# GpSimd is asked first for three steps of the first eight weight pieces, with 40 unread transpositions and new planner constants

## The chip, the cores and the metric

One core of one Trainium2 chip runs the kernel. The metric is the device time of one execution in microseconds (us), the median of three runs.

## What is computed

An attention with a decay bias, a network with a squared relu, and a network that takes the maximum of three products. All of it is done at float32 accuracy.

```python
def _attn_ref(q, k, v, s):                       # q, k, v: 4 x 8 x 576 x 64
    scores = scale * np.matmul(q, k.transpose(0, 1, 3, 2))
    cum = np.cumsum(np.maximum(s, 0.0), axis=-1)
    bias = -(cum[:, :, :, None] - cum[:, :, None, :])
    scores = np.where(causal, -1000000000.0, scores + np.minimum(bias, 0.0))
    attn = np.exp(scores - np.max(scores, axis=-1, keepdims=True))
    attn = attn / (np.sum(attn, axis=-1, keepdims=True) + 1e-09)
    return np.matmul(attn, v)

def _moe_ref(x, w_in, w_out, s, b):              # 2304 x 512, 512 x 2048, 2048 x 512
    r = np.maximum(x @ w_in, 0.0)
    return (s * (r * r) + b) @ w_out

def _moe2_ref(x, w1, w2, w3, w_out):             # three 512 x 768, then 768 x 512
    return np.maximum(np.maximum(x @ w1, x @ w2), x @ w3) @ w_out
...
x = attn_out.transpose(0, 2, 1, 3).reshape(B * S, H * D)
return _moe2_ref(_moe_ref(x))                    # 2304 x 512
```

## The kernel before

**Arithmetic.** TensorE multiplies float32 in a fast form (fp32r) that keeps only part of the digits. A number x is therefore held as a high part and a low part, and a product is three matmuls (L286 to L288: high x high, high x low, low x high). Attention scores of the first two kinds of jobs are made in plain float32 (L581, L583).

**Weights.** They come as 64-bit floats. `weight_steps` (L300) turns a piece of 128 rows into a high and a low float32 tile in nine steps: 0 the load (L311, SP's queue), 1 a scaling of the upper 32-bit words (L316, on ScalarE), 2 and 3 bit operations (L319, L321, VectorE), 4 the rounding to the high part (L275 or L277, ScalarE or VectorE), 5 and 6 bits and product of the lower words (L325, L327, VectorE), 7 a difference (L282) and 8 a sum that gives the low part (L331). Steps 7 and 8 are done on VectorE or GpSimd. The first network's weights in 14 pieces (name "a") are staged in tiles `wg`, `stage` and `wst`; the first eight, 384 columns wide, make `wa_in`, the other six, 512 wide, make `wa_out`.

**Attention.** Jobs of two heads: four jobs A (first 320 rows), four jobs B (the other 256), then whole pairs (W). For each block of rows: scores into PSUM (`ps`, L581/L583, later L591), a minimum on VectorE that also copies the scores to `pp` (L602), the exponential on ScalarE (L608), transpositions of `pp` on TensorE (`pt`, L680), copies of `pt` out of PSUM (L275 on ScalarE, L279 on VectorE), the product with v (`px`, L699), and a product with reciprocal sums (L707). The result `x` is split in high and low (L275, L282) for the first network, whose matmuls (L286 to L288) run in the same time as the attention. Each job needs its q and k (`raw`, L513), a one-hot row (`oh`, L571, on GpSimd), and the decay table (`dd`, L562; `dm`, L482, L484, L277, L275, saved by L493 and L494).

**Order.** Every engine runs its own list of instructions in a fixed order. A planner in the kernel (`Plan`) makes these lists at build time: it walks through the steps in an assumed time, gives each engine the ready step of the lowest priority, and takes a step's costs, its due time and the landing of loads from the constants at the top of the file. A step whose costs are a table of engines goes to the first engine named, unless another would end it earlier by `LATE_0` (`LATE` later in the plan, `LATE_F` for urgent steps). `convert` (L918) lists the steps of a weight piece; its due times are `W_1`, `W_S1`, `W_2` and `W_S2` with `W_AT`.

**Unread transpositions.** `warm` (L547) issues 30 transpositions of the identity before the first data come. `keep` (L553) is a step of the lowest priority, one transposition into a bank of PSUM that nobody reads; the planner puts it where TensorE has no other step. `KEEPS` of them exist, 56.

Of the kernel before, what the change touches and what calls it, by code (L numbers as in the profile page):

```python
# [8 lines left out]
F32 = mybir.dt.float32  # L9
# [4 lines left out]
AF = mybir.ActivationFunctionType  # L14
# [18 lines left out]
KEEP = 1  # L33
KEEPS = 56
VIA = 4
# [12 lines left out]
TURN = -6.0  # L48
LEAST = -0.257
EXP = 0.52  # L50
D_T = 1.77
P_HI = 0.517
R_AT = 0.543
D_AV = 5.833
# [3 lines left out]
AV = {"A": ((0, 1, 2),), "B": ((0, 1, 2), (3, 4)), "W": ((0, 1, 2), (3, 4))}  # L58
W_1 = -2.561
W_S1 = 4.286  # L60
W_2 = 29.555
W_S2 = 1.679
WG = (0, 1, 2, 5, 6)
WX = (7, 10, 13)
WB_1 = 116.522
WB_S = 8.739
WO_AT = 0.055
W_AT = (0, 2.0, 2.3, 2.8, 2.9, 3.3)
SLACK = 0.039
LATE = 0.898  # L70
LATE_F = 1.001
LATE_0 = 0.158
BUSY = 150
# [3 lines left out]
FAR_R = 0.846  # L77
FAR_Q = 0.818
LOADED = (60, 260)
# [4 lines left out]
TURN_C = 0.08  # L84
AV_C = 0.002
TURNS = ("turn_p", "turn_r")
# [140 lines left out]
def fused_kernel(ctx, tc, q, k, v, s, w_in, w_out, ms, mb, w1, w2, w3, w_fin, out,  # L227
                 f_split=6):
    nc = tc.nc
# [23 lines left out]
    scale = 1.0 / float(D) ** 0.5  # L253
# [46 lines left out]
    def weight_steps(piece, stage_tile):  # L300
# [10 lines left out]
        nc.sync.dma_start(st.bitcast(I64), src)  # L311
        yield
        word = lambda dt, i: st.bitcast(dt).rearrange("p (n t) -> p n t", t=2)[:, :, i]
        a = stage_tile(step, "wsa")
        lo = a.bitcast(F32R) if lo is None else lo
        nc.scalar.activation(a, word(F32, 1), AF.Copy, scale=2.0 ** -112)  # L316
        yield
# [600 lines left out]
    def convert(name, z, piece, stage_tile, prios, needs, ring_st, ring_a, **k):  # L918

        state = []  # L920

        def step(on=None):
            if not state:
                state.append(side_steps(piece) if name == "s" else weight_steps(piece(), stage_tile))
                next(state[0])
            else:
                state[0].send(on)

        n = piece.n
        either2 = {"DVE": dve(n), "Pool": pool_(n)}  # L930
        shift, either = dve_fast(n) - 0.06, {"Pool": pool_(n), "DVE": dve(n)}
        back = [("save", z)] if name == "s" else [("savef", z, 0), ("savef", z, 1)] if name == "f" else [("w", name, z, 8)]
        parts = (("SP", (1, 2 * n), (), [(ring_st, back)]), ("ACT", act(n), (0,), [(ring_a, back)] if ring_a else []),
                 ("DVE", shift, (1,), []), ("DVE", dve(n), (2,), []), ({"ACT": act(n), "DVE": dve_fast(n) - 0.06}, 0, (3,), []),
                 ("DVE", shift, (4,), []), ("DVE", dve(n), (5,), []), (either2, 0, (6,), []), (either2, 0, (7,), []))
        for i, (engine, cost, after, take) in enumerate(parts):
            if name in ("a", "s") and i == 1:
                cost += 0.05
            if name == "s":
                if engine == "DVE":  # L940
                    cost += 0.05
                elif isinstance(engine, dict) and "DVE" in engine:
                    engine = engine | {"DVE": engine["DVE"] + 0.05}
            add(("w", name, z, i), engine, cost, prios[min(i, len(prios) - 1)], [("w", name, z, j) for j in after] + (needs if not i else []), step, take=take,
                **(k | {"delay": 1.0} if name == "f" and not i else k))
# [14 lines left out]
    for z, piece in enumerate(all_a):  # L960
# [12 lines left out]
        t = W_1 + z * W_S1 if z < 4 else W_2 + (z - 4) * W_S2  # L973
        convert("a", z, piece, stage_a, [t + d for d in W_AT], [], "wg" if z in WG else "wx" if z in WX else "ws", None, att=True)

# [326 lines left out]
    def word(q, x, dt, i):  # L1302
        return wsts[q, x].bitcast(dt).rearrange("p (n t) -> p n t", t=2)[:, :, i]
# [393 lines left out]
```

## Time and profile before

| | us |
|---|---|
| median of 3 runs | 864.92 |
| lowest and highest | 864.79, 864.97 |
| the profiled execution | 864.14 |
| its span | 862.4 |
| busy TensorE (PE) | 853.8 |
| busy VectorE (DVE) | 633.7 |
| busy ScalarE (ACT) | 473.4 |
| busy GpSimd (POOL) | 333.4 |

The profile shows one execution. Its times are in us from the start of the span unless ns is written. A line number is that of the kernel; helpers such as `copy` (L275 to L279) and `minus` (L282) have one line for many uses, so the tiles' names tell the uses apart. An instruction's length overlaps with the next one's start by some 0.1 us, so what an instruction takes from its engine is better read from one start to the next. The granted clock of TensorE is at its full level, 2.4 GHz, in every stretch shown.

### The profile page before, as it was taken

To read this page: it belongs to the slowest core of one execution; us is meant where nothing else is said; L and a number is where in the kernel's file an instruction comes from. 1 tells how busy PE (TensorE), PEld (TensorE's weight loads), DVE (VectorE), ACT (ScalarE), POOL (GpSimd) and SP (SyncE) were. 2 spreads that over 40 slices of the span, in tenths; PEclk is the share of its full clock that TensorE was granted. 3 is DMA by queue.
4 is the path that set the end of the run, shared out by engine and by line. 5 is a ranking of instruction groups with operands and counts; after the bars stand their busy time and mean duration, and the time that the engine had idled before them with its cause. 6 is when DMAs were issued, how large, how long until landed. Compare 5 with 4: busy or idle time off the path is not lost.

```text
span 862.4 us, 15613 instructions
## 1 busy us (share of the span) xinstructions
PE 853.8 (99%) x5064; PEld 769.4 (89%) x5064; DVE 633.7 (73%) x1554; ACT 473.4 (55%) x1175; POOL 333.4 (39%) x353
## 2 busy tenths in 40 slices
PE   8999999999999999999999999999999999999998
PEld 7678989888888999999988888889998999989996
DVE  7999799878787789859599896454668366836650
ACT  7988998999885444726264462551236223532221
POOL 3536676687635222705041241410228122702220
PEclk9999999999999999999999999999999999999999
DMA  7664756656753576665759686428885255615502
GB/s 215 196 195 129 236 179 193 216 163 199 241 162 126 166 235 213 199 217 169 231 158 298 204 290 216 138 94 307 315 295 202 89 169 180 221 74 171 171 25 74
DMA packets 111336, 163.25 MB, mean 189 GB/s; under 512 B 11048, under 2 KB 62616, under 8 KB 111256
## 3 DMA queue, kind: packets, MB, share of 16 engines
q1 hardware_dynamic: 111016, 161.98, 58.1%
q8 instruction: 41, 0.67, 0.3%
q14 instruction: 39, 0.32, 0.1%
q10 hardware_dynamic: 240, 0.28, 0.1%
HBM read 117.79 MB, written 44.43 MB: 188 GB/s over the span
## 4 chain that ended last, share of the span: by engine, by line
PE 94%; DVE 3%; DMA 1%; ACT 1%; issue 0%; SPq 0%; ACTq 0%; DVEq 0%
PE mm L286 26%; PE mm L288 26%; PE mm L287 26%; PE pt L680 6%; PE px L699 5%; PE ps L591 5%; PE ps L581 1%; DMA wst<-in_moe_w_in_dram 1%; DVE pp L602 1%; PE pr L628 0%; DMA s<-in_s_dram 0%; SPq L513 0%; DVE stage L282 0%; DMA raw<-in_q_dram 0%; ACT pp L608 0%
## 5 line engine op out<-in xcount | busy, mean ns | idle before, releaser
L282 POOL TENSOR_TENSOR gbl<-g,gbh 128x512 fp32r<-128x512 f32 (+1 forms) x50 | 64.1, 1282 | 146.5 <-ACT gbh L275 143.5
L1141 ACT ACTIVATE g<-g 128x512 f32<-128x512 f32 (+4 forms) x86 | 48.3, 561 | 77.5 <-DVE g L1137 77.2
L608 ACT ACTIVATE pp<-pp,mn 64x64 f32<-64x64 f32 (+4 forms) x160 | 88.3, 553 | 4.4 <-DVE mn L602 4.1
L282 POOL TENSOR_TENSOR set<-raw,set 64x384 fp32r<-64x384 f32 x72 | 76.3, 1085 | 23.7 <-PE ps L591 6.3
L286 PE MATMUL mm<-ty,sdp 128*128 128x384 f32 x252 | 84.3, 335 | 0.0
L288 PE MATMUL mm<-ty,sdp 128*128 128x384 f32 x252 | 84.3, 335 | 0.0
L287 PE MATMUL mm<-ty,sdp 128*128 128x384 f32 x252 | 84.3, 334 | 0.0
L1137 DVE TENSOR_SCALAR g<-mm 128x512 f32<-128x512 f32 (+4 forms) x86 | 51.8, 602 | 41.8 <-PE mm L288 39.8
L680 PE MATMUL pt<-ident,pp 128*128 128x128 f32 x480 | 75.3, 276 | 1.9 <-DVE mn L602 1.5
L288 PE MATMUL mm<-gbh,wb_out 128*128 128x512 f32 (+2 forms) x200 | 73.7, 368 | 0.0
L286 PE MATMUL mm<-gbh,wb_out 128*128 128x512 f32 (+2 forms) x200 | 73.7, 368 | 0.0
L287 PE MATMUL mm<-gbl,wb_out 128*128 128x512 f32 (+2 forms) x200 | 73.7, 368 | 0.0
L288 PE MATMUL mm<-xa,wb_in 128*128 128x512 f32 (+1 forms) x200 | 73.5, 368 | 0.0
L287 PE MATMUL mm<-xa,wb_in 128*128 128x512 f32 (+1 forms) x200 | 73.5, 368 | 0.0
L286 PE MATMUL mm<-xa,wb_in 128*128 128x512 f32 (+1 forms) x200 | 73.5, 367 | 0.0
L275 ACT ACTIVATE pt<-pt 128x384 f32<-128x384 f32 (+3 forms) x158 | 62.7, 425 | 11.8 <-PE pt L680 10.2
L602 DVE CUSTOM_DVE_ANT_0 pp<-late_keys,ps 64x64 f32<-64x64 f32 (+4 forms) x160 | 62.2, 418 | 8.8 <-PE ps L591 7.1
L680 PEld LDWEIGHTS pt<-ident,pp 128*128 128x128 f32 x480 | 56.0, 140 | 10.7 <-ACT pp L608 2.5
L282 POOL TENSOR_TENSOR ga<-g,ga 128x448 fp32r<-128x448 f32 (+3 forms) x36 | 41.0, 1138 | 60.0 <-ACT ga L275 58.1
L591 PE MATMUL ps<-set 128*128 128x288 f32 (+4 forms) x288 | 53.4, 314 | 0.0
L286 PE MATMUL mm<-ga,wa_out 128*128 128x448 f32 (+3 forms) x144 | 51.4, 357 | 0.0
L699 PE MATMUL px<-pt,vn 128*64 128x256 f32 (+3 forms) x512 | 51.2, 340 | 0.0
(269 smaller groups left out, 2417.7 us busy)
## 6 DMA issues: line engine op xcount, KB each, us to landing
sdp<-s_d SPq DMA_DIRECT2D x126, 256.0 KB
s_d<-sdp SPq DMA_DIRECT2D x42, 384.0 KB
wst<-in_moe_w_dram SPq DMA_DIRECT2D x24, 384.0 KB
wst<-in_moe_w_out_dram SPq DMA_DIRECT2D x32, 256.0 KB
raw<-in_q_dram SPq DMA_DIRECT2D x24, 288.0 KB
raw<-in_k_dram SPq DMA_DIRECT2D x24, 288.0 KB
bl<-y_d SPq DMA_DIRECT2D x24, 192.0 KB
out_dram<-o SPq DMA_DIRECT2D x17, 256.0 KB
```

Of the source, the lines that this page charges most:

```text
L275: nc.scalar.activation(dst, src, AF.Copy, scale=1.0 if scale is None else scale)
L282: ENGINES[on].tensor_tensor(dst, a, b, op=ALU.subtract)
L286: nc.tensor.matmul(ps, lhs[0], rhs[0], start=first, stop=False)
L287: nc.tensor.matmul(ps, lhs[0], rhs[1], start=False, stop=False)
L288: nc.tensor.matmul(ps, lhs[1], rhs[0], start=False, stop=last)
L591: nc.tensor.matmul(ps[:, :k1 - k0], t[:, a, QS[i]:QS[i] + P], t[:, b, k0:k1], start=x == 0, stop=x == 1)
L602: nc.vector.tensor_tensor_reduce(out=pp[j][i][:n, k0:k1], in0=late_keys[:n, a:a + k1 - k0], in1=ps_.pop((job.n, u, j))[:n, :k1 - k0], scal ...
L608: nc.scalar.activation(p[:n, :w], p[:n, :w], AF.Exp, bias=mns[job.n, j][:n, i:i + 1], scale=-1.0, accum_out=sums[job.n % 2][:n, j, i:i + 1])
L680: nc.tensor.transpose(pt[:, c - c0, :], pp[j][i][:, c * P:(c + 1) * P], ident)
L699: nc.tensor.matmul(px_[job.n][hf][j * D:(j + 1) * D, a0 - h0:h1 - h0], vn[job.n % 2][:, c, j, :], columns(job, pr["p", job.n, j], c, c + 1 ...
L1137: nc.vector.tensor_scalar(st["g", f], st["u", f][:, :n], 0.0, None, op0=ALU.max)
L1141: nc.scalar.activation(st["g", f], st["g", f], AF.Square)
```

## The change

1. A string `A_ON` has four letters for each of the 14 first pieces, for the steps 1, 4, 7 and 8. "q" asks for GpSimd first and then the other engine, "b" leaves it as it was. The first eight pieces have "qbqq": scaling, difference and sum are asked of GpSimd first, the rounding is as before. Piece 10 has one "q", for its difference. Step 1 goes through `copy`, so its line is now that of a helper.
2. `KEEPS` is 40.
3. Eight of the planner's other constants change, among them the due times of the weight pieces and the surcharge for a step on its second engine. `A_D` shifts the due times of the pieces 10 and 13.

```diff
-KEEPS = 56
+KEEPS = 40
...
-LEAST = -0.257
+LEAST = -0.584
...
-R_AT = 0.543
+R_AT = 1.57
...
-W_1 = -2.561
+W_1 = -1.649
...
-W_S2 = 1.679
+W_S2 = 0.568
...
+A_ON = 'qbqqqbqqqbqqqbqqqbqqqbqqqbqqqbqqbbbbbbbbbbqbbbbbbbbbbbbb'
+A_D = (0.0, 0.0, 0.0, 0.0, 0.0, 0.0, 0.0, 0.0, 0.0, 0.0, -1.463, 0.0, 0.0, -1.181)
...
-LATE = 0.898
+LATE = 0.981
...
-LATE_0 = 0.158
+LATE_0 = 0.453
...
-FAR_Q = 0.818
+FAR_Q = 1.221
...
-AV_C = 0.002
+AV_C = 0.012
...
-        yield
+        on = yield
...
-        nc.scalar.activation(a, word(F32, 1), AF.Copy, scale=2.0 ** -112)
+        copy(a, word(F32, 1), on or "ACT", 2.0 ** -112)
...
+        on = lambda i, d=either2: {e: d[e] for e in {"b": d, "p": ("Pool",), "q": ("Pool", *(x for x in d if x != "Pool"))}[A_ON[4 * z + i] if name == "a" else "b"]}
```

The lines behind the changed ones move down by two, from `weight_steps` to the middle of `convert`, and by three after it (L282 is then L284, L602 is L604).

GpSimd's list from the one-hot row of job 2 on, before (`oh` rows of the jobs, `xa` low parts of attention results, `stage`, `wg` and `wa_in` steps 7 and 8 of weight pieces):

```order
L571 CAST oh<-rows 128x128 x2
L501 MEMSET set 64x1152 x2
L571 CAST oh<-rows 128x128
L282 TENSOR_TENSOR xa<-x_507,xa 128x320
L282 TENSOR_TENSOR xa<-x_660,xa 128x320
L282 TENSOR_TENSOR stage<-stage,wa_in 128x384
L331 TENSOR_TENSOR wa_in<-stage 128x384
L571 CAST oh<-rows 128x128
L282 TENSOR_TENSOR xa<-x_729,xa 128x320
L282 TENSOR_TENSOR wg<-wg,wa_in 128x384
L571 CAST oh<-rows 128x128
L282 TENSOR_TENSOR stage<-stage,wa_in 128x384
```

and now:

```order
L573 CAST oh<-rows 128x128
L279 TENSOR_SCALAR wg<-wg 128x384 x3
L279 TENSOR_SCALAR stage<-stage 128x384
L284 TENSOR_TENSOR wg<-wg,wa_in 128x384
L333 TENSOR_TENSOR wa_in<-wg 128x384
L573 CAST oh<-rows 128x128
L284 TENSOR_TENSOR wg<-wg,wa_in 128x384
L503 MEMSET set 64x1152
L333 TENSOR_TENSOR wa_in<-wg 128x384
L503 MEMSET set 64x1152
L284 TENSOR_TENSOR wg<-wg,wa_in 128x384
L333 TENSOR_TENSOR wa_in<-wg 128x384
```

Four scalings and three whole pairs of difference and sum now stand before and between the one-hot rows of the jobs 3 and 4, where two one-hot rows and two fills stood.

TensorE's list from job 0's widest transpositions to the product with v, before (`warm` are unread transpositions, `ps` job 1's scores, `pr` the transposed reciprocal sums):

```order
L680 MATMUL pt<-ident,pp_1_156 128x128 x2
L553 MATMUL warm<-ident 128x128 x28
L680 MATMUL pt<-ident,pp_2_152 128x128 x3
L680 MATMUL pt<-ident,pp_2_157 128x128 x3
L553 MATMUL warm<-ident 128x128
L581 MATMUL ps<-raw 128x64 x2
L583 MATMUL ps<-dd,oh 128x64 x2
L553 MATMUL warm<-ident 128x128 x8
L628 MATMUL pr<-ident,rr 128x128
L553 MATMUL warm<-ident 128x128 x3
L699 MATMUL px<-pt,vn_117 64x320 x2
```

and now:

```order
L682 MATMUL pt<-ident,pp_1_156 128x128 x2
L555 MATMUL warm<-ident 128x128 x12
L682 MATMUL pt<-ident,pp_2_152 128x128 x3
L682 MATMUL pt<-ident,pp_2_157 128x128 x3
L555 MATMUL warm<-ident 128x128 x2
L583 MATMUL ps<-raw 128x64 x2
L585 MATMUL ps<-dd,oh 128x64 x2
L555 MATMUL warm<-ident 128x128 x4
L583 MATMUL ps<-raw 128x192 x2
L585 MATMUL ps<-dd,oh 128x192 x2
L682 MATMUL pt<-ident,pp_0_150 128x128
```

12 instead of 28 unread transpositions stand ahead of job 0's widest ones, and job 1's scores of 192 columns have moved ahead of the reciprocal sums and of the product with v. Up to job 2's first scores the lists hold the same work, with 56 unread transpositions before and 39 now.

SP's queue of loads around those of job 2, before (`wst` is the fifth weight piece, `raw` q and k):

```order
L311 DMA stage<-in_moe_w_in_dram 128x384 x2
L513 DMA raw<-in_q_dram 64x320 x2
L513 DMA raw<-in_k_dram 64x320 x2
L311 DMA wst<-in_moe_w_in_dram 128x384
L311 DMA wg<-in_moe_w_in_dram 128x384
```

and now:

```order
L313 DMA stage<-in_moe_w_in_dram 128x384 x2
L313 DMA wst<-in_moe_w_in_dram 128x384
L515 DMA raw<-in_q_dram 64x320 x2
L515 DMA raw<-in_k_dram 64x320 x2
L495 DMA dm_d<-dm 32x1152
```

The fifth weight piece is loaded ahead of job 2's q and k, and the sixth has moved behind the saving of the decay table.

## Rows read from the trace of the kernel before

**Rows 1.** Page, busy time, share and instructions of each engine.

```profile
PE 853.8 (99%) x5064; PEld 769.4 (89%) x5064; DVE 633.7 (73%) x1554; ACT 473.4 (55%) x1175; POOL 333.4 (39%) x353
```

**Rows 2.** Stretches: us; busy us (instructions) of PE, PEld, DVE, ACT, POOL; clock; DMA.

```profile
10.00:22.33 12.33, 12.04 (x108) 10.46 (x108) 11.79 (x42) 11.92 (x41) 0.31 (x2) 1.00 0.87 265
22.33:60.00 37.67, 36.02 (x277) 26.34 (x277) 36.58 (x118) 34.53 (x107) 18.73 (x20) 1.00 0.63 189
60.00:265.00 205.00, 204.33 (x1578) 176.79 (x1577) 172.93 (x569) 181.74 (x524) 130.14 (x140) 1.00 0.61 190
265.00:862.00 597.00, 593.75 (x3058) 548.95 (x3056) 406.19 (x806) 240.31 (x494) 177.36 (x162) 1.00 0.57 188
```

**Rows 3.** Timeline, TensorE: start, length, engine, line, operation, count, [idle before <-releaser].

```profile
10.29 0.30 PE L680 MATMUL pt<-ident,pp 128*128 128x128 f32 x1 [0.70 <-DVE mn L602]
...
11.73 3.22 PE L553 MATMUL warm<-ident 128*128 128x128 f32 x28
14.79 0.82 PE L680 MATMUL pt<-ident,pp 128*128 128x128 f32 x6
...
22.33 0.57 PE L581 MATMUL ps<-raw 64*128 64x64 f32 x3
```

**Rows 4.** Timeline, ScalarE.

```profile
13.29 0.55 ACT L316 ACTIVATE wg<-wg 128x384 f32<-128x384 f32 x1
13.76 0.51 ACT L275 ACTIVATE wa_in<-wg 128x384 fp32r<-128x384 f32 x1
...
18.30 0.76 ACT L275 ACTIVATE dm<-dm 32x64 fp32r<-32x64 f32 x2
```

**Rows 5.** GpSimd by form, 0 to 60 us: busy us, mean ns, idle before.

```profile
L571 POOL CAST oh<-rows 128x128 fp32r<-128x128 f32 x8 | 3.4, 421 | 17.8 <-PE ps L583 15.3 <-DVE wg L321 2.5
...
L282 POOL TENSOR_TENSOR stage<-stage,wa_in 128x384 f32<-128x384 f32 x2 | 2.0, 1004 | 0.7 <-DVE stage L325 0.7
...
L331 POOL TENSOR_TENSOR wa_in<-stage 128x384 fp32r<-128x384 f32 x1 | 1.2, 1207 | 0.6 <-POOL stage L282 0.6
...
L436 POOL CAST pick<-either 128x640 fp32r<-128x640 f32 x1 | 0.7, 716 | 0.0
```

**Rows 6.** Timeline, VectorE, first 22 us.

```profile
10.33 0.48 DVE L602 CUSTOM_DVE_ANT_0 pp<-late_keys,ps 128x320 f32<-128x320 f32 x1
...
11.15 0.74 DVE L484 SCALAR_TENSOR_TENSOR dm<-s,dm 32x576 fp32r<-32x576 f32 x1
...
17.25 0.55 DVE L282 TENSOR_TENSOR wg<-wg,wa_in 128x384 f32<-128x384 f32 x1
17.72 0.20 DVE L602 CUSTOM_DVE_ANT_0 pp<-late_keys,ps 64x64 f32<-64x64 f32 x1
...
20.89 0.49 DVE L707 TENSOR_TENSOR x<-px,rb 128x320 f32<-128x320 f32 x1
...
21.76 0.48 DVE L602 CUSTOM_DVE_ANT_0 pp<-late_keys,ps 128x320 f32<-128x320 f32 x1
```

**Rows 7.** Timeline, GpSimd, then VectorE, at 33 us.

```profile
33.21 1.00 POOL L282 TENSOR_TENSOR stage<-stage,wa_in 128x384 f32<-128x384 f32 x1 [0.67 <-DVE stage L325]
...
33.25 1.39 DVE L327 SCALAR_TENSOR_TENSOR stage<-stage 128x384 f32<-128x384 uint32 x1
```

**Rows 8.** VectorE by form, 0 to 60 us: busy us, mean ns, idle before.

```profile
L327 DVE SCALAR_TENSOR_TENSOR wg<-wg 128x384 f32<-128x384 uint32 x5 | 3.3, 652 | 0.0
L331 DVE TENSOR_TENSOR wa_in<-wg 128x384 fp32r<-128x384 f32 x5 | 2.7, 548 | 0.0
...
L327 DVE SCALAR_TENSOR_TENSOR stage<-stage 128x384 f32<-128x384 uint32 x2 | 2.0, 980 | 0.0
...
L282 DVE TENSOR_TENSOR stage<-stage,wa_in 128x384 f32<-128x384 f32 x1 | 0.9, 936 | 0.0
```

**Rows 9.** The chain that ended last, 8 to 30 us: start, length, what.

```profile
14.32 5.61 DMA wst<-in_moe_w_in_dram
...
19.96 0.57 ACT stage L316
```

## What I expect, before the run

> **What bounds the kernel now.** I read the busy times first, then the table of stretches, then the timelines of the first 60 us. TensorE is busy for 853.8 of 862.4 us [rows 1]. From 60 to 265 us it is busy for 204.33 of 205 us, and after that it lacks some 3 us of 597, at the very end [rows 2]. So from 60 us on TensorE itself is the bound, and the change takes no arithmetic from it. Counted in the two orders, TensorE's instructions are the same, kind by kind, but for 16 transpositions that nobody reads. What the change can win lies before 60 us, and it has two forms there. The unread transpositions: 55 of the 56 run between 10 and 22.33 us, and 28 of them in a row take from 11.73 to 14.79 us, 0.109 us each, so all 56 are 6.1 us of TensorE's time [rows 3]. And open idle time: 0.70 us before the first transposition of a softmax, 0.29 us from 10 to 22.33 us in part the same, and 1.65 us from 22.33 to 60 us [rows 2, 3]. That is some 8 us which TensorE spends waiting for others, filled or not.
>
> For whom it waits: VectorE is busy for 11.79 of 12.33 us and 36.58 of 37.67 us in the two stretches, ScalarE for 11.92 and 34.53 us, GpSimd for 0.31 and 18.73 us [rows 2]. VectorE all but never stands still. So the softmax chain (VectorE's minimum, ScalarE's exponential) shares two full engines with the conversion of the weights, and GpSimd has room. An instruction taken from VectorE or ScalarE here is on the path.
>
> **The change, part by part.** *Scaling.* The planner gives 5 of 8 scalings to GpSimd, 3 stay on ScalarE. One costs ScalarE 0.47 us: it starts at 13.29 us and the next instruction starts at 13.76 us [rows 4]. ScalarE loses 5 x 0.47 = 2.35 us. On GpSimd a scaling of this form does not occur before. From below, the one-input copies there: 128 columns take 0.42 us in the mean of eight and 640 take 0.72 us, which puts 384 at 0.57 us; from above, the two-input form of 384 columns at 1.00 us [rows 5]. I take 0.75 us, nearer to the copies because there is one input: 3.75 us more on GpSimd (2.9 to 5.0).
>
> *Difference and sum.* GpSimd took 4 of 8 differences and 2 of 8 sums; now it takes all 16. That is 10 instructions off VectorE. One is 0.55 us long and the next instruction starts 0.47 us after it (17.25 to 17.72 us), so VectorE gains 10 x 0.47 = 4.7 us [rows 6]. On GpSimd they add 4 x 1.0 and 6 x 1.2 us = 11.2 us [rows 5].
>
> *What GpSimd's work does to VectorE.* GpSimd gets 15 instructions and 15 us more, in a stretch where it has 19.0 us of work in 50. That fits, but the two engines hold each other up. At 33.21 us GpSimd starts a difference of 1.00 us, and a VectorE instruction that starts at 33.25 us takes 1.39 us where the undisturbed two-input form takes 0.55 us [rows 7, 8]. From below: three groups in the first 60 us show 5 x 0.10, 2 x 0.43 and 0.39 us over that form, together 1.8 us, over 20 GpSimd instructions after 22.33 us, 0.09 us each [rows 2, 8]. From above: every added instruction catches a step of VectorE half way through a hold like that of 1.39 - 0.55 = 0.84 us, 0.42 us each. With 15 added instructions that is 1.4 to 6.3 us; the steps that remain on VectorE (four of each piece) stand closer together than before, so I take 0.2 us each, 3.0 us, nearer to the end that was measured in this place. VectorE is left with -4.7 + 3.0 = -1.7 us (-3.3 to +1.6), ScalarE with -2.35 us.
>
> The Trainium skill, page "SBUF — State Buffer", section "Who interferes with whom", speaks against this change: the port pair that VectorE and GpSimd share is an exclusive lock, the loser blocks for the whole instruction, and two-input steps on SBUF are among those that take it. The trace agrees with it at 33.25 us; applied to each added instruction it gives the upper end, and so the slower rival below.
>
> *The unread transpositions.* 40 instead of 56: 16 x 0.109 = 1.74 us less on TensorE, if the data come so much sooner; otherwise TensorE is idle for the same time. What brings them sooner is seen at job 2's first product, which starts at 22.33 us [rows 3]. In both orders the same work stands before it on TensorE, with 56 unread ones before and 39 now, so it is due at 22.33 - 17 x 0.109 = 20.5 us. Three suppliers must make that. VectorE: from job 0's widest minimum (10.33 us) to job 1's widest (21.76 us) it had 35 instructions for 11.4 us; now there are 26. Eight conversion steps are gone (six with two inputs at 0.47 us, two shorter ones, some 3.3 us), and the product with the reciprocal sums (0.5 us); a step of the decay table (0.7 us) now stands ahead of the first of these minima instead of behind it; a copy out of PSUM is new (some 0.4 us, an estimate from the two-input step of 0.47 us). Job 1's widest minimum is then due 3.5 us sooner, less at most 3 us of holds [rows 6]. ScalarE: two scalings that stood before job 0's copies out of PSUM are gone from there (0.9 us), and 0.7 us of the decay table's copies come in [rows 4]. The first weight piece's rounding, which stands between these copies, now waits for a GpSimd scaling and two VectorE steps; behind it are queued job 0's other copies, so up to 0.8 us can come back here. The queue of SP: the fifth weight load is now issued ahead of job 2's four loads. Before, it was issued at 14.32 us, after them, and landed 5.61 us later, at 19.9 us [rows 9]. With the places exchanged job 2's data land at about that time. This keeps 20.5 us possible, and leaves nothing much below it.
>
> *All else.* After 60 us a few copies move from VectorE to ScalarE and the other way; their cover is that TensorE has product work of the first network in its queue there and stands still for 0.67 us in 205 [rows 2]. If that cover failed, each would cost its 0.4 to 0.5 us. The other constants move priorities; I cost them at nothing for the same reason. From 22.33 to 60 us both full engines have less to do, and I let 0.3 of the 1.65 us of idle time go.
>
> **Sum.** -1.74 - 0.3 = -2.0 us. The profiled execution took 864.14 us with a span of 862.4 us, so 1.74 us lie around the span; it would be 862.1 us. The median of the three runs is 864.92 us, 0.8 us above the profiled one; against it the forecast is 862.9 us.
>
> **Rivals.** *A: waits take the place of the unread transpositions.* The rounding of the first piece and what is queued behind it on ScalarE come late, and TensorE stands idle for the 1.74 us that it no longer fills. For it: a chain of GpSimd, VectorE and ScalarE replaces one of two engines, and the loads end at 19.9 us. Against: 35 VectorE instructions become 26. Time 864.9 us (864.2 to 865.6).
>
> *B: the hold decides.* Each of GpSimd's 15 added instructions stops a two-input step of VectorE for 0.42 us, 6.3 us against 4.7 us won, and GpSimd's scalings are at the dear end, 5.0 us instead of 3.75, of which a quarter reaches the chain. VectorE is full, so its 1.6 us and those 0.3 us go to TensorE's idle time between 22 and 60 us, beside the unread ones that turn into waits: 864.92 + 1.9 = 866.8 us. It decides from 4.7 / 15 = 0.31 us per instruction on; the trace shows 0.09.
>
> *C: more is won.* The idle time from 22.33 to 60 us goes too, because VectorE is no longer the later one: 864.92 - 1.74 - 1.65 = 861.5 us, 861.2 at best with the 0.3 us before. Against: ScalarE is as full as VectorE.
>
> That GpSimd does not take what it is asked for is no rival: its order shows 21 of the 24 steps.
>
> **How the numbers follow.** Forecast 0.48 (862.0 to 863.8 us), A 0.30, B 0.12, C 0.10. A measurement can tell 0.2% from no change, which is 863.2 and 866.65 us. Of the forecast 0.35 lie below 863.2: faster 0.35 + 0.10 = 0.45, same 0.13 + 0.30 = 0.43, slower 0.12. The range from 861.4 to 866.0 us leaves out B and a little of C.
>
> **What would show it.** Right: job 2's first product near 20.5 us; VectorE's busy time down by 1 to 3 us over the first 60 us; GpSimd's up by 13 to 16 us; idle time of TensorE from 10 to 60 us no more than 2 us. A: the same idle time plus 1.7 us, ended by ScalarE. B: VectorE's sums of the steps at L325, L327 (L327, L329 after) grow by 5 us or more. It is wrong altogether if TensorE's busy share from 60 to 265 us falls, or if a GpSimd scaling takes over 1 us.

## The result and the profile after

The changed kernel took 871.13 us in the median (869.74 to 872.27), the kernel before 864.86 us: a ratio of 1.0069 (95% interval 1.0057 to 1.0082), 6.3 us slower. Once more on the same chip as the first experiments it was 870.17 us against 865.24 us, 1.0056 (1.0032 to 1.0080), with executions from 867.5 to 874.7 us where the kernel before stays between 864.6 and 866.7 us. The profiled execution took 869.74 us, its span 867.9 us, 5.5 us more than before. Forecast were 862.9 us (861.4 to 866.0).

The page, busy time, share and instructions of each engine, against [rows 1]:

```profile
PE 855.2 (99%) x5048; PEld 767.8 (88%) x5048; DVE 634.3 (73%) x1523; ACT 477.4 (55%) x1189; POOL 349.9 (40%) x370
```

TensorE has its 16 instructions less, as counted. GpSimd has 16.5 us more work, 14.3 us of it in the first 60 us, where 15 were forecast. Where the time went is read from four stretches. The columns are those of [rows 2]: the stretch, its length, then busy us and instructions of PE, PEld, DVE, ACT, POOL, clock, DMA. First the kernel before (its second stretch stands in [rows 2]), then the changed one:

```profile
0.00:22.33 22.33, 19.73 (x157) 17.26 (x157) 17.96 (x65) 16.80 (x52) 7.15 (x33) 1.00 0.71 213
...
60.00:100.00 40.00, 39.76 (x305) 33.84 (x305) 34.18 (x102) 34.63 (x93) 19.85 (x20) 1.00 0.56 172
100.00:265.00 165.00, 164.57 (x1277) 142.96 (x1274) 138.75 (x468) 147.11 (x432) 110.29 (x121) 1.00 0.62 194
```

```profile
0.00:22.33 22.33, 18.66 (x139) 15.73 (x139) 16.71 (x59) 14.97 (x48) 16.09 (x41) 1.00 0.72 212
22.33:60.00 37.67, 35.04 (x266) 25.23 (x264) 34.43 (x101) 33.08 (x102) 24.12 (x26) 1.00 0.57 166
60.00:100.00 40.00, 37.83 (x272) 31.62 (x270) 34.90 (x94) 31.14 (x80) 19.35 (x19) 1.00 0.58 185
100.00:265.00 165.00, 164.31 (x1276) 143.01 (x1275) 133.59 (x448) 150.40 (x449) 109.47 (x121) 1.00 0.60 186
```

Take the unread transpositions off TensorE's counts (all 56 by 22.33 us before; 39 of 40 by then after). Before, 101 instructions that matter are done by 22.33 us, 378 by 60, 683 by 100 and 1960 by 265 us; after, 100, 365, 637 and 1913. So the changed kernel is level at 22.33 us, 13 behind at 60, 46 behind at 100 and 47 at 265 us. At 164.57 / 1277 = 0.129 us each, 47 instructions are 6.1 us (an estimate, since the instructions are of unequal length), about the 5.5 us of the span. 33 of the 47 are lost between 60 and 100 us, where the prediction had put nothing. The granted clock is 1.00 in all four stretches, so this execution lost its time without the clock. VectorE is no longer full in the second stretch: 34.43 us where it had 36.58.

TensorE's timeline, with the idle time ahead and what ended it. Early waits:

```profile
19.31 0.33 PE L682 MATMUL pt<-ident,pp 128*128 128x128 f32 x1 [0.64 <-ACT pt L277]
...
19.79 0.81 PE L583 MATMUL ps<-raw 64*128 64x320 f32 x4
...
22.39 0.44 PE L583 MATMUL ps<-raw 64*128 64x64 f32 x4
...
26.63 0.33 PE L630 MATMUL pr<-ident,rr 128*128 128x128 f32 x1 [0.40 <-DVE rr L626]
...
27.64 0.44 PE L682 MATMUL pt<-ident,pp 128*128 128x128 f32 x2 [0.27 <-ACT pt L277]
28.81 0.52 PE L672 MATMUL pr<-rt,pick 128*128 128x64 f32 x3 [0.73 <-DVE rt L664]
...
30.90 0.84 PE L583 MATMUL ps<-raw 64*128 64x192 f32 x3 [0.43 <-DVE mn L604]
```

Job 2's first product starts at 22.39 us, as in the kernel before (22.33 us, [rows 3]), with 17 unread transpositions fewer ahead of it; then come waits for VectorE and ScalarE. In the trace of after_again, the same kernel once more, the wait at 19.31 us is missing and the product starts at 21.57 us; the span is 867.7 us all the same. And late ones:

```profile
74.35 0.41 PE L290 MATMUL mm<-ga,wa_out 128*128 128x320 f32 x1 [0.33 <-DVE wa_out L333]
...
78.56 0.30 PE L630 MATMUL pr<-ident,rw 128*128 128x128 f32 x1 [0.49 <-DVE rw L623]
...
81.20 0.42 PE L290 MATMUL mm<-ga,wa_out 128*128 128x320 f32 x1 [0.45 <-DVE wa_out L333]
...
98.95 1.36 PE L593 MATMUL ps<-set 128*128 128x64 f32 x7 [0.57 <-DMA set<-dm_d]
```

TensorE waits for low parts of the first network's second weights (`wa_out`), for a reciprocal, and for a load of the decay table. VectorE's last sum of such a weight piece, before and after, and on SP's queue the load that it needs, before and after:

```profile
78.20 1.25 DVE L331 TENSOR_TENSOR wa_out<-stage,wst 128x512 fp32r<-128x512 f32 x1
```

```profile
87.20 1.34 DVE L333 TENSOR_TENSOR wa_out<-stage,wst 128x512 fp32r<-128x512 f32 x1
```

```profile
62.45 1.64 SPq L311 DMA_DIRECT2D wst<-in_moe_w_out_dram  x1
```

```profile
74.33 0.33 SPq L313 DMA_DIRECT2D wst<-in_moe_w_out_dram  x1
```

The last load is issued 12 us later, and the last piece is ready at 88.5 us instead of 79.4.

GpSimd's added steps by form, 0 to 60 us, against [rows 5], then two of VectorE's steps (busy us, mean ns); L329 is L327 of [rows 8], and for the shift the row of before follows:

```profile
L279 POOL TENSOR_SCALAR wg<-wg 128x384 f32<-128x384 f32 x4 | 5.9, 1503 | 0.3 <-DMA wg<-in_moe_w_in_dram 0.3
L284 POOL TENSOR_TENSOR wg<-wg,wa_in 128x384 f32<-128x384 f32 x5 | 5.4, 1076 | 2.5 <-ACT pp L610 1.9 <-DVE wg L327 0.6
L333 POOL TENSOR_TENSOR wa_in<-wg 128x384 fp32r<-128x384 f32 x5 | 5.3, 1050 | 1.2 <-DVE wg L329 0.6 <-POOL wg L284 0.6
...
L279 POOL TENSOR_SCALAR stage<-stage 128x384 f32<-128x384 f32 x1 | 1.2, 1188 | 1.5 <-DMA stage<-in_moe_w_in_dram 1.5
```

```profile
L329 DVE SCALAR_TENSOR_TENSOR wg<-wg 128x384 f32<-128x384 uint32 x5 | 5.3, 1060 | 0.0
L321 DVE TENSOR_SCALAR wg<-wg 128x384 int32<-128x384 int32 x5 | 4.0, 801 | 0.3 <-POOL wg L279 0.3
```

```profile
L319 DVE TENSOR_SCALAR wg<-wg 128x384 int32<-128x384 int32 x5 | 1.7, 349 | 0.1
```

A scaling took 1.50 us in the mean of four and 1.19 us in one, 7.2 us for the five, 1.44 us each. VectorE's product is 1.06 us long where it was 0.65, its shift 0.80 us where it was 0.35. One case, GpSimd and then VectorE:

```profile
23.07 1.00 POOL L333 TENSOR_TENSOR wa_in<-wg 128x384 fp32r<-128x384 f32 x1
24.02 1.05 POOL L503 MEMSET set<- 64x1152 f32 x1
```

```profile
23.23 2.06 DVE L321 TENSOR_SCALAR wg<-wg 128x384 int32<-128x384 int32 x1
```

The shift starts 0.16 us after a GpSimd sum and lasts 2.06 us, until the fill behind that sum is over too: by its times, one VectorE step stood through two GpSimd instructions.

### The profile page after: what moved, and what is told of

Its sections match the earlier page's. It is cut to its first block, busy times and chain, and to the rows that moved or that the text cites. A ratio compares the mean times of both kernels' runs of the same rounds, so it can differ in the third digit from the quotient of the medians.

```text
span 867.9 us, 15562 instructions
## 1 busy us (share of the span) xinstructions
PE 855.2 (99%) x5048; PEld 767.8 (88%) x5048; DVE 634.3 (73%) x1523; ACT 477.4 (55%) x1189; POOL 349.9 (40%) x370
## 4 chain that ended last, share of the span: by engine, by line
PE 92%; DVE 3%; DMA 2%; SPq 1%; issue 1%; ACT 0%; ACTq 0%
PE mm L288 26%; PE mm L290 25%; PE mm L289 25%; PE pt L682 5%; PE px L701 5%; PE ps L593 4%; DMA set<-dm_d 1%; DMA stage<-in_moe_w_in_dram 1%; PE ps L583 1%; DVE pp L604 1%; SPq L515 1%; DVE stage L323 0%; PE pr L630 0%; DVE wg L321 0%; SPq L313 0%
## 5 line engine op out<-in xcount | busy, mean ns | idle before, releaser
L284 POOL TENSOR_TENSOR gbl<-g,gbh 128x512 fp32r<-128x512 f32 (+1 forms) x50 | 65.0, 1301 | 129.6 <-ACT gbh L277 127.3
L284 POOL TENSOR_TENSOR set<-raw,set 64x384 fp32r<-64x384 f32 x72 | 75.1, 1069 | 31.8 <-ACT set L277 17.0
L288 PE MATMUL mm<-ty,sdp 128*128 128x384 f32 x252 | 84.2, 334 | 0.0
L289 PE MATMUL mm<-ty,sdp 128*128 128x384 f32 x252 | 84.2, 334 | 0.0
L290 PE MATMUL mm<-ty,sdp 128*128 128x384 f32 x252 | 84.2, 334 | 0.0
L604 DVE CUSTOM_DVE_ANT_0 pp<-late_keys,ps 64x64 f32<-64x64 f32 (+4 forms) x160 | 62.6, 419 | 16.9 <-PE ps L593 10.0
L277 ACT ACTIVATE pt<-pt 128x256 f32<-128x256 f32 (+3 forms) x169 | 67.0, 424 | 11.8 <-PE pt L682 10.3
L284 POOL TENSOR_TENSOR ga<-g,ga 128x448 fp32r<-128x448 f32 (+3 forms) x36 | 39.7, 1102 | 76.6 <-ACT ga L277 74.8
```

Source lines behind the costliest of these rows:

```text
L277: nc.scalar.activation(dst, src, AF.Copy, scale=1.0 if scale is None else scale)
L284: ENGINES[on].tensor_tensor(dst, a, b, op=ALU.subtract)
L288: nc.tensor.matmul(ps, lhs[0], rhs[0], start=first, stop=False)
L289: nc.tensor.matmul(ps, lhs[0], rhs[1], start=False, stop=False)
L290: nc.tensor.matmul(ps, lhs[1], rhs[0], start=False, stop=last)
L604: nc.vector.tensor_tensor_reduce(out=pp[j][i][:n, k0:k1], in0=late_keys[:n, a:a + k1 - k0], in1=ps_.pop((job.n, u, j))[:n, :k1 - k0], scal ...
```

## The experiments

Theories. **H**: GpSimd's added work holds VectorE, and that is dear. **L**: a piece's chain got longer, by the scaling above all. **C**: the new constants (or the order that they make) are at fault, whichever engine does the steps. **W**: the unread transpositions only fill waits; **K**: they keep TensorE's clock up. **G**: asking for GpSimd is at fault by the order that it makes. **R**: any order other than the one selected is some us slower.

In the last column of this table stands what VectorE's steps from 10 to 60 us took over the shortest of the same form, summed where it is over 0.1 us, worked out from the trace ("held"). All ratios are against runs of the kernel before on the same chip.

| run | us | ratio (95%) | held, us |
|---|---|---|---|
| before | 865.0 to 865.2 | 1 | 3.0 |
| after_again | 870.17 | 1.0056 (1.0032 to 1.0080) | 7.1 |
| e_scale_act | 871.22 | 1.0068 (1.0050 to 1.0086) | 6.4 |
| e_sumdiff_dve | 867.84 | 1.0029 (1.0016 to 1.0043) | 3.3 |
| e_all_back | 868.90 | 1.0043 (1.0026 to 1.0059) | 1.7 |
| e_as_before | 868.67 | 1.0039 (1.0024 to 1.0054) | 3.1 |
| a_keeps56 | 870.69 | 1.0063 (1.0051 to 1.0076) | 7.0 |
| keeps_only | 865.40 | 1.0008 (0.9999 to 1.0017) | 3.0 |
| b_unread_pool | 870.29 | 1.0062 (1.0047 to 1.0077) | 8.3 |
| b_scale_pool | 865.90 | 1.0010 (1.0001 to 1.0020) | 4.6 |
| ask_only | 872.41 | 1.0082 (1.0068 to 1.0096) | 7.1 |
| consts_only | 869.96 | 1.0054 (1.0041 to 1.0068) | 2.9 |
| consts56 | 870.12 | 1.0052 (1.0035 to 1.0068) | 2.4 |
| early_only | 865.83 | 1.0008 (0.9998 to 1.0017) | 2.7 |
| late_only | 864.72 | 0.9996 (0.9986 to 1.0005) | 3.6 |
| avc_only | 864.83 | 0.9999 (0.9990 to 1.0008) | 2.9 |
| late0_late_avc | 864.80 | 0.9995 (0.9985 to 1.0004) | 3.3 |
| late0_only | 863.46 | 0.9982 (0.9972 to 0.9991) | 3.0 |
| late0_keeps40 | 863.49 | 0.9985 (0.9976 to 0.9995) | 3.1 |

### The changed kernel's order, with steps given back

> The changed kernel once more, beside the kernel before on the same chip, as the base for the three runs after it. All theories: 871 us (869.5 to 872.5), some 6 us above the kernel before.

The next four keep every engine's list as the planner made it and change only which engine issues a step, at the same place:

```diff
-                state[0].send(on)
+                state[0].send(MOVED.get((z, i), on) if name == "a" else on)
```

`MOVED` is a table by piece and step. For e_scale_act it gives ScalarE for step 1 of the pieces 0, 1, 2, 3 and 5:

> The changed kernel with its order kept as it is, but the five scalings that its order gives to GpSimd are issued on ScalarE, each at the same place of the order. Theory L (the chain of a weight piece got longer: the scaling takes 1.44 us on GpSimd instead of 0.47 us, so the staging tiles come free later and the last pieces are late): the first products of job 2 come some 2 us sooner and the time falls by 2 to 5 us, to 866 to 869 us. Theory C (the new constants made an order that is slow with either engine): within 1 us of the changed kernel. Theory H (GpSimd's two-input steps hold VectorE): falls by no more than 1.5 us, since the sums and differences are still there.

For e_sumdiff_dve, VectorE for the steps 7 and 8 of the first eight pieces:

> The changed kernel with its order kept, but the sixteen differences and sums of the first eight pieces are issued on VectorE at the same places; the scalings stay on GpSimd. VectorE gets 16 x 0.47 = 7.5 us of work more before 60 us. Theory H (holds): VectorE's stretched steps shrink by 4 us or more, and the time falls by 2 us or more. Theory L with the scaling as the main cause: no faster than the changed kernel, 870 to 874 us, since VectorE is full. Theory C: within 1 us of the changed kernel or slower.

For e_all_back both:

> Both of the last two edits together: the changed kernel's order and its 40 unread transpositions, with nothing more on GpSimd than ScalarE and VectorE can take back. Theory C: 870 us or more, because the order itself is at fault. Theory L or H: below 868 us, though VectorE has 7.5 us and ScalarE 2.4 us more to do than the order assumes.

For e_as_before both, but the six differences and sums that GpSimd has in the kernel before stay there:

> The changed kernel's order and its 40 unread transpositions, but every engine does the steps that it does in the kernel before: the scalings on ScalarE, ten differences and sums back on VectorE, six on GpSimd. What is left over the kernel before is the price of the order alone. If the order costs nothing by itself: 864 to 866 us. If it is at fault: 867 us or more, with TensorE idle for 2 us or more between 60 and 100 us, as with all sixteen on VectorE.

L falls: with the scalings back on ScalarE the time is 871.2 us, not 866 to 869, and in the pair without GpSimd's sums 868.9 against 867.8 us. No gain shows from giving them back, though a scaling is three times as long on GpSimd. H is borne out in part: the sums and differences back on VectorE are worth 2.3 us in both pairs (870.17 to 867.84, 871.22 to 868.90), although VectorE then has up to 7.5 us more work; the intervals within each pair overlap at their edges, so it is the two pairs together that say it. Part of it goes with TensorE's clock: the mean granted clock was 0.998 or less in 3 of 6 and 2 of 4 executions with the sums on GpSimd, and in none of 5 and 1 of 6 without them. The other executions differ by less, 868.1 against 867.8 us and 869.9 against 868.9 us in the medians. So what the hold costs without the clock isn't shown. C holds for the larger part: when every engine does the steps that it does in the kernel before, 3.7 us of loss are left where after_again has 4.9 us, at a mean clock of 1.0 in all four executions. The stretches of e_as_before and its late waits on TensorE:

```profile
22.33:60.00 37.67, 35.85 (x274) 25.87 (x275) 35.51 (x112) 32.91 (x102) 15.69 (x18) 1.00 0.56 166
60.00:100.00 40.00, 37.64 (x266) 31.62 (x265) 34.71 (x95) 31.92 (x82) 19.16 (x18) 1.00 0.60 185
```

```profile
73.18 0.41 PE L290 MATMUL mm<-ga,wa_out 128*128 128x320 f32 x1 [0.32 <-DVE wa_out L333]
...
80.03 0.41 PE L290 MATMUL mm<-ga,wa_out 128*128 128x320 f32 x1 [0.45 <-DVE wa_out L333]
```

VectorE's held time is as before (3.1 us), yet from 60 to 100 us TensorE is busy for 37.64 us instead of 39.76, and it waits for the same things as in the changed kernel. That part of the loss lies in the order. e_all_back, where VectorE has the most to do, lies at 868.9 us, between the theories' forecasts, and decides between none of them by itself.

### The unread transpositions

```diff
-KEEPS = 56
+KEEPS = 40
```

> The kernel before with 40 unread transpositions instead of 56 (the last 16, which stand from job 1's first scores on), all else in its order. Theory W (waits take their place): 865.2 us, within 0.4 us of the kernel before, and TensorE idle for some 1.7 us more between 15 and 23 us. The forecast's step (they cost 0.109 us each): 863.5 us. Theory K (they keep TensorE's clock up): some executions show a granted clock below 0.999 and take 1 to 4 us longer.

```diff
-        for _ in range(KEEP):
+        for _ in range(KEEP + (x >= 24)):
```

> The changed kernel with its last 16 unread transpositions issued twice, so 56 in all, its order kept. Theory K: the executions with a granted clock below 0.999 vanish, the spread shrinks to 3 us, and the median is 1 us or more below that of the changed kernel, in spite of 1.7 us more work. Theory W: within 1 us of the changed kernel's 870 us, with the same spread. If they cost their own time: 872 us.

W holds, and the forecast's step falls. In the kernel before, the 16 that were left out become waits, by TensorE's timeline (before, the 16 ran from 16 to 22 us, two of them from 19.87 us and three from 20.22 us):

```profile
19.56 0.33 PE L682 MATMUL pt<-ident,pp 128*128 128x128 f32 x1 [0.74 <-ACT pp L610]
...
20.65 0.33 PE L682 MATMUL pt<-ident,pp 128*128 128x128 f32 x1 [0.48 <-ACT pt L277]
```

The median is the same within 0.2%. In the changed kernel 16 more cost nothing that can be told either (870.69 against 870.17 us). K isn't decided. With 40, in orders about as fast as that of before, 3 of 21 executions had a mean granted clock of 0.998 or less: one of keeps_only (0.996, 869.1 us, where the others of its eleven end by 866.4 us) and two of late0_keeps40, below (0.998 and 0.995, 865.4 and 865.5 us, where its others end by 863.8 us). With 56, the kernel before has one such in 90 (0.998, at 867.1 us its slowest), and early_only, below, one in ten (0.997, 866.8 us). If there is a price, it is paid in some executions and not in the median.

### GpSimd's work alone

b_unread_pool adds to the kernel before five scalings and ten sums on GpSimd, into a tile (`unread`) that nobody reads:

```diff
+        copy(a, word(F32, 1), on or "ACT", 2.0 ** -112); extra = lambda v: step == 384 and v == "DVE" and nc.gpsimd.tensor_tensor(unread, a, a, op=ALU.add)
...
+        minus(a, a, hi.bitcast(F32), on); extra(on)
...
+        ENGINES[on].tensor_tensor(lo, a, g, op=ALU.add); extra(on)
...
+                state[0].send(on); name == "a" and i == 1 and z in (0, 1, 2, 3, 5) and nc.gpsimd.tensor_scalar(unread, late_keys[:, :384], 2.0, None, op0=ALU.mult)
```

> The kernel before in its own order, with 15 instructions more on GpSimd whose results nobody reads: five scalings of 128x384, where five pieces are scaled, and ten two-input sums, where VectorE does its ten differences and sums. Nothing waits for them but GpSimd's own queue. Theory H (GpSimd's work holds VectorE, and that alone costs time): VectorE's steps from 10 to 60 us are stretched by 3 to 5 us more than in the kernel before, and the time grows by 1 to 4 us, to 866 to 869 us. Without it: within 0.5 us of 865.2 us.

5.2 us slower, more than the 1 to 4 us that H gave. VectorE is held for 8.3 us instead of 3.0, and does all its old work besides. The stretch in which it happens:

```profile
22.33:60.00 37.67, 33.44 (x235) 24.09 (x234) 36.79 (x107) 30.93 (x93) 25.03 (x28) 0.91 0.53 157
```

All of it is lost between 22.33 and 60 us, where TensorE gets 42 instructions fewer done (235 instead of 277) and the granted clock is 0.91 in the mean. Closer, with TensorE's timeline below it:

```profile
24.00:26.00 2.00, 0.72 (x9) 0.45 (x5) 2.00 (x6) 1.28 (x6) 0.94 (x2) 1.00 0.66 209
26.00:28.00 2.00, 1.91 (x12) 1.26 (x10) 2.00 (x10) 1.98 (x9) 1.90 (x3) 0.60 0.39 114
28.00:30.00 2.00, 2.00 (x12) 0.86 (x10) 2.00 (x2) 1.11 (x5) 2.00 (x3) 0.55 0.07 9
```

```profile
25.64 1.57 PE L682 MATMUL pt<-ident,pp 128*128 128x128 f32 x7 [1.27 <-DVE mn L604]
27.14 1.44 PE L583 MATMUL ps<-raw 64*128 64x320 f32 x4
```

From 24 to 26 us TensorE is busy for 0.72 of 2 us and waits for VectorE's minimum; from 26 to 30 us the granted clock is 0.60 and 0.55, so for most of the time at the lower of its two levels. Four products of 64x320 take 1.44 us at 27.14 us; the same four take 0.81 us at 19.79 us in the changed kernel (its timeline above). It falls once more, to 0.66 and 0.50 from 36 to 40 us. In the mean of the stretch 0.09 of 37.67 us are lost, 3.4 us of full clock, so a part of this execution's loss can be the clock's, and it fell after a wait. But of the four executions three have a mean clock of 0.996, and the fourth, with 0.999, took 870.46 us, no less. The experiment can't part the hold from GpSimd's own queue either: a one-hot row that GpSimd starts at 21.75 us in the kernel before starts at 24.53 us here, behind unread work.

> The kernel before in its own order, with the five scalings of the change issued on GpSimd in place of ScalarE. If a scaling of 1.2 to 1.8 us on GpSimd sits in the path of a piece: 866.5 us or more, and job 2's first product later than 22.33 us by 1 us. If ScalarE's relief of 2.4 us outweighs it, as the runs with the changed kernel's order hint: 864 to 865.2 us.

The scalings alone cost 0.8 us in the kernel before, between the two forecasts. GpSimd's timeline there:

```profile
10.27 5.55 POOL L279 TENSOR_SCALAR wg<-wg 128x384 f32<-128x384 f32 x3
16.29 3.52 POOL L279 TENSOR_SCALAR stage<-stage 128x384 f32<-128x384 f32 x1 [0.47 <-DMA stage<-in_moe_w_in_dram]
```

Three scalings from 10.27 us take 5.55 us and the next one alone 3.52 us, beside VectorE steps that follow one another without a gap (busy for 12.24 of 12.33 us). The hold goes both ways.

### The order alone

```diff
-A_ON = 'qbqqqbqqqbqqqbqqqbqqqbqqqbqqqbqqbbbbbbbbbbqbbbbbbbbbbbbb'
+A_ON = 'bbbbbbbbbbbbbbbbbbbbbbbbbbbbbbbbbbbbbbbbbbbbbbbbbbbbbbbb'
```

> The changed kernel with no step asked of GpSimd (the string all b), with its constants and its 40 unread transpositions; the order is planned anew. Theory C (the constants are at fault): 868 us or more, with the last pieces of the first network's weights done after 84 us and TensorE idle for 2 us or more from 60 to 100 us. Theory G (asking for GpSimd is at fault, by the order that it makes): 864 to 866 us, as before.

> The constants and the 56 unread transpositions of the kernel before, with the string that asks for GpSimd; the order is planned anew. Theory G: 868 us or more. Theory C: 864 to 867 us.

Each is slow by itself, so neither G nor C is the cause alone: ask_only loses 7.2 us with the old constants, consts_only 4.8 us without anything asked of GpSimd. Together, in the changed kernel, they cost no more than the constants alone (ratios 1.0056 and 1.0054). ask_only loses it from 60 to 100 us: TensorE gets 240 instructions done there (305 in the kernel before) and is busy for 35.60 us at a mean clock of 0.91. The clock fell in all four of its executions (means of 0.996 to 0.998); 0.09 of 40 us is 3.6 us of full clock, so up to half of its loss can be the clock's. consts_only has nothing of GpSimd's and yet loses in the same places:

```profile
22.33:60.00 37.67, 35.77 (x262) 26.22 (x261) 36.10 (x111) 31.64 (x96) 12.66 (x16) 1.00 0.58 170
60.00:100.00 40.00, 38.42 (x291) 31.19 (x291) 35.03 (x103) 35.48 (x98) 15.89 (x18) 1.00 0.58 185
```

Its longest waits there are for ScalarE, for an exponential and for a copy out of PSUM:

```profile
71.39 0.55 PE L682 MATMUL pt<-ident,pp 128*128 128x128 f32 x3 [0.38 <-ACT pp L610]
...
73.64 0.44 PE L682 MATMUL pt<-ident,pp 128*128 128x128 f32 x2 [0.48 <-ACT pt L277]
```

With 56 unread transpositions and the same order otherwise:

> The changed constants with nothing asked of GpSimd, as in the run before that took 870.0 us, but with 56 unread transpositions; the rest of the order is the same. If they only fill waits: 869.5 to 871 us. If the missing 16 are why the two halves of the constants (865.8 and 864.7 us, with 56) cost 4.8 us together: 866 us or less.

870.12 us: they fill waits there too.

The constants in two halves, one of those that move steps before 30 us, one of the others:

> The kernel before with the four changed constants that move steps before 30 us (LEAST, R_AT, W_1, FAR_Q), nothing asked of GpSimd, 56 unread transpositions. If the slowness of the new constants comes from the start of the order: 868 to 871 us, as with all of them. If from the later ones: 864.5 to 866 us.

> The kernel before with the other changed constants (W_S2, A_D, LATE, LATE_0, AV_C): the order is the same up to 32 us. If the due times of the later weight pieces are at fault: 867 us or more, with TensorE idle for 2 us or more between 60 and 100 us. If the start of the order is: 863 to 865.5 us, since LATE_0 alone made it 1.7 us faster.

Neither half is slow; all eight together are. Single ones:

```diff
-LATE_0 = 0.158
+LATE_0 = 0.453
```

> The kernel before with one of the eight changed constants, the surcharge for a step on its second engine (0.453 instead of 0.158): the order is the same up to 46 us and another one after it, GpSimd is asked for nothing, and the planner's own assumed end is 0.1 us earlier. Theory R (an order that differs from the one that was selected is some us slower, and the planner's assumed times don't tell): 867 us or more. If only the asking and the early order cost time: 864.5 to 865.8 us.

> The kernel before with another of the eight constants alone (the addition of 0.012 instead of 0.002 us that decides between products with v and transpositions): the order is the same up to 37 us and differs little after it; the planner's assumed end is 0.2 us later. Theory R: 866 us or more. Otherwise 864.8 to 865.8 us.

> The kernel before with three of the changed constants, LATE, LATE_0 and AV_C; due times, start of the order and GpSimd's work as before. If the surcharge's gain is its own: 863 to 864.5 us. If each new order differs by some us either way: anywhere from 862 to 868 us.

> The kernel before with the surcharge of 0.453 and 40 unread transpositions. If these only fill waits, as in the kernel before: 863.5 us, within 0.4 us of the surcharge alone.

R falls as it was put: a new order isn't slower as such. The surcharge alone makes the kernel 1.7 us faster than before, 0.9982 (0.9972 to 0.9991), clear of no change though not of 0.2%; with 40 unread transpositions it is the same. The sets that hold the surcharge with others are back at the kernel before (0.9996 and 0.9995), and all together cost 4.8 us. What late0_only shows: TensorE is busy from 60 to 100 us without a gap, and the last weight piece is early. Its stretch, and VectorE's last sum:

```profile
60.00:100.00 40.00, 40.00 (x308) 34.12 (x305) 31.29 (x91) 34.61 (x94) 20.88 (x22) 1.00 0.56 176
```

```profile
77.69 1.43 DVE L333 TENSOR_TENSOR wa_out<-stage,wst 128x512 fp32r<-128x512 f32 x1
```

When that last sum ends, in the trace of each kernel, and the kernel's time:

| kernel | last piece ready, us | time, us |
|---|---|---|
| late0_only | 79.1 | 863.5 |
| avc_only | 79.3 | 864.8 |
| before | 79.4 | 865.0 to 865.2 |
| late_only | 80.6 | 864.7 |
| late0_late_avc | 81.2 | 864.8 |
| early_only | 84.2 | 865.8 |
| consts56 | 84.4 | 870.1 |
| b_unread_pool | 85.1 | 870.3 |
| consts_only | 85.4 | 870.0 |
| e_all_back | 86.5 | 868.9 |
| e_as_before | 87.4 | 868.7 |
| e_sumdiff_dve | 87.5 | 867.8 |
| e_scale_act | 87.9 | 871.2 |
| the changed kernel | 88.5 | 870.2 to 871.1 |
| ask_only | 90.7 | 872.4 |

Orders with the piece ready by 81.2 us are as fast as before or faster, orders with it after 85 us lose 2.6 to 7.2 us. But a late piece isn't the common cause. early_only has it at 84.2 us, within 0.8 us of the kernel before in its time, and TensorE doesn't stand still from 60 to 100 us:

```profile
60.00:100.00 40.00, 40.00 (x307) 34.65 (x307) 33.72 (x107) 34.14 (x92) 17.28 (x20) 1.00 0.61 187
```

consts56 has it 0.2 us later and loses 5.1 us. In b_unread_pool, with the order of before, the piece is late because time was lost before 60 us: from 60 to 100 us TensorE is busy for 39.77 us. And in consts_only none of TensorE's waits of 0.15 us or more from 60 to 100 us is ended by a weight piece. Only in the changed kernel's order and in ask_only does TensorE wait for `wa_out`, and no run moved that piece by itself. Left open is which steps of a slow order make TensorE wait. Of all versions run, late0_only and late0_keeps40 are the fastest, ahead of both kernels.

## Why the prediction was wrong, point by point

**What bounds the kernel.** Right at the start, wrong in what was drawn from it. TensorE was the bound from 60 us on in the kernel before, and so "all else" was costed at nothing, with 0.67 us of idle time in 205 us as the cover. That is the step that failed. The cover was a property of the old order. In the new one TensorE's idle time from 60 to 265 us is 2.86 us, and 33 of the 47 instructions are lost there; e_as_before, with every step on its old engine, shows 3.7 us as the price of the order alone. Why that order makes TensorE wait is known only wait by wait (for `wa_out`, a reciprocal, a load); the step that causes them stays open. Both of the prediction's signs of being wrong altogether came ("if TensorE's busy share from 60 to 265 us falls, or if a GpSimd scaling takes over 1 us"); it had given neither a chance of its own.

**Unread transpositions.** 1.74 us were forecast as a gain; in the median they are worth nothing that can be told (keeps_only, a_keeps56, consts56, late0_keeps40). That is what rival A said of this term: waits take their place. Job 2's first product was due at 20.5 us and came at 22.39, or at 21.57 in after_again. In the first of these traces GpSimd's first scaling kept VectorE waiting until 12.32 us (0.30 us), where the same shift starts at 11.82 us in the kernel before; the rounding that waits for both held ScalarE, as the prediction had seen; what it hadn't is that a scaling that stays on ScalarE now stands ahead of two copies that TensorE needs, while its load is on the way. ScalarE's timeline:

```profile
14.57 0.52 ACT L277 ACTIVATE wa_in<-wg 128x384 fp32r<-128x384 f32 x1 [0.39 <-DVE wg L323]
...
18.43 0.55 ACT L277 ACTIVATE stage<-stage 128x384 f32<-128x384 f32 x1 [1.44 <-DMA stage<-in_moe_w_in_dram]
```

1.44 us of waiting for the load at 18.43 us, then 0.64 us of TensorE at 19.31 us. I had followed SP's queue for job 2's data only. In after_again the same scaling starts at 16.99 us and these waits are missing; but the granted clock is 0.95 there from 22.33 to 60 us, and by 60 us both traces have as much done (366 and 365 instructions, counted as above). What these waits cost isn't shown.

**Scaling.** 0.75 us (0.57 to 1.00) was taken; measured were 1.19 us at the least and 1.44 us in the mean, 7.2 us for the five where 2.9 to 5.0 were allowed. The term was mis-sized by nearly half and didn't decide: b_scale_pool costs 0.8 us, and in the changed order the scalings' engine makes no difference that shows.

**Difference and sum.** VectorE's 10 instructions less are as counted, GpSimd's 1.0 to 1.1 us each too.

**The hold.** 4.1 us more than before (7.1 against 3.0; 7.6 in the first profile), 0.27 to 0.31 us for each of 15 instructions, where 0.20 was taken and 0.09 was the trace's. That 0.09 counted three kinds of steps; over all of VectorE's steps, as in the table, the kernel before has 3.0 us for 22 GpSimd instructions from 10 to 60 us, 0.14 us each. The measured hold lies inside the bounds, and near the point that rival B named (0.31 us). Its sum assumed that VectorE stays full and pays only the difference. But VectorE has less to do (45.0 us busy from 10 to 60 us where it had 48.4), and TensorE still waits for it; that each hold falls on one step of a chain is argued, not shown. In b_unread_pool 5.3 us more hold stand beside 5.2 us more time, on a VectorE whose list didn't change; GpSimd's own queue and the clock have a part in that which isn't known. In "what would show it", VectorE's busy time down by 1 to 3 us was listed as a sign of being right; it fell by 3.4 us over the first 60 us, and the time rose.

The Trainium skill, page "SBUF — State Buffer", section "Who interferes with whom", speaks of an exclusive lock in which the order of issue, not the shape, decides who blocks. The traces show blocking on both sides, and through more than one instruction: 2.06 us for a shift of 0.35 us on VectorE, 3.52 us for a scaling of 1.19 us on GpSimd. Taken as a rule for each added instruction it would have given 866.8 us, rival B, nearer than the forecast.

**Rivals.** A was given 0.30 and is right for the transpositions alone (keeps_only, 865.4 us against 865.2 us). B was given 0.12; its hold is there, at about the size that it named, but that it decides isn't shown. Both at once, and an order that costs 3.7 us by itself, were in no case. The rivals were worked out one by one against the old order, and the change made a new one.

## What to carry to other kernels

When a change makes a planner lay out a static order anew, the idle time of the old trace is no bound for the new one: look in the new order for what the bound engine would wait for (a load, a converted weight, a copy on another engine), and give the order a price of its own, of both signs. Moving work from a full engine to an idle one that shares a resource with it has to be costed with what the two engines do to each other. Unread work on the idle engine gives a first measure of that, though its own queue and the clock come into it: here it cost 5.2 us. Filler work that only stood in waits gained nothing in the median when it was left out.

## What the runs showed of the hardware

A multiplication by a constant on GpSimd, 128x384 float32 with every second word read, takes at least 1.19 us, longer than its two-input sum of the same size (1.00 us); with the words side by side it took at least 1.17 us (b_unread_pool). VectorE and GpSimd hold each other: a VectorE step was stretched to 2.06 us through two GpSimd instructions, a GpSimd scaling to 3.52 us (b_scale_pool) and to 5.63 us (b_unread_pool, from 13.47 us).

TensorE's granted clock fell after short waits in the changed kernel too. Three stretches of after_again:

```profile
26.00:28.00 2.00, 1.31 (x11) 0.95 (x11) 1.94 (x3) 1.30 (x5) 1.26 (x2) 1.00 0.04 0
28.00:30.00 2.00, 1.57 (x16) 1.27 (x13) 1.97 (x11) 1.85 (x6) 1.37 (x3) 0.89 0.69 269
30.00:32.00 2.00, 2.00 (x11) 1.72 (x9) 1.24 (x6) 1.40 (x7) 2.00 (x3) 0.50 1.10 340
```

From 26 to 28 us TensorE is busy for 1.31 of 2 us and the clock is 1.00; in the two stretches behind it is 0.89 and then 0.50, TensorE being busy all the time in the last. The executions of the changed kernel spread over 7 us, those of the kernel before over 3 us. Of its ten executions the five with a mean granted clock below 0.999 took 869.5 to 874.7 us, the five others 867.5 to 870.9 us. So the clock makes a part of the spread, and the kernel is slower than before without it too.
